# Banded attention into an ELU feed-forward on one core: a planned order of the first transfers, and two leading 256-token tiles with x transposed on TensorE

## The chip, the core and the metric

One core of one Trainium2 chip runs the whole program. The metric is the device time in microseconds of one execution; a run's time holds the profiled span of the instructions and a little around it. Three runs of the kernel before took 389.42, 391.37 and 386.51 us.

## What is computed

Eight batches of eight heads, 576 tokens, head width 64, float32 inputs. Attention inside a band of 32 positions to either side, then the heads side by side as 4608 tokens of width 512, then a feed-forward with an ELU between two matrices (512 to 2048 to 512).

```python
scores = scale * np.matmul(q, k.transpose(0, 1, 3, 2))
mask = np.abs(pos[:, None] - pos[None, :]) <= 32
attn = softmax(np.where(mask, scores, -1e9))
x = np.matmul(attn, v).transpose(0, 2, 1, 3).reshape(4608, 512)
h = x @ w_in
g = np.where(h > 0.0, h, np.exp(np.minimum(h, 0.0)) - 1.0)
out = g @ w_out
```

## The kernel before

**Tiling.** A *pair* is 128 tokens (two query blocks of 64); there are 36. For a pair, QK (line 216, 16 small matmuls into psS), SM (line 227, exp on ACT), MK (line 239, the band mask on DVE, two instructions), AV (line 251, two groups of eight matmuls, with a column of ones that gives the row sum), RN (lines 264 and 266, reciprocal and multiply on DVE, once for each group, giving xs) and X (line 275, a DMA transpose on SP's queue from xs into xt). Four pairs make an FFN *tile* of 512 tokens, nine tiles in all (`sizes = [4] * 9`). For a tile, sixteen steps H (line 286, four matmuls 128x512 into psH), EX (line 294, exp on ACT), FF and GG (lines 300 and 305, on DVE), then Y (line 319, four parts of four matmuls for each 128 tokens), YC (line 325, ACT copy) and OUT (line 330, SP).

**Loads.** q and k of a batch come in four float32 transfers (line 151: k and q of four heads, then of the other four); batch 0's are issued on SP, later ones on ACT's queue. POOL casts them to bf16 (line 166; batch 0's are shared with ACT and DVE), PE transposes them (T, line 176), ACT and DVE copy them out (E, lines 189 and 191). v of a batch is five casting transfers on POOL's queue (lines 197 to 202), and two transfers on SP's queue (SV, lines 206 and 207) make a copy of v shifted by 64 partitions, which the odd query blocks read. w_in and w_out come in four chunks each (lines 351 and 356), also on POOL's queue. Chunk c of w_in serves steps 4c to 4c+3 of H; chunk c of w_out serves part c of Y.

**What sets the order.** `Plan` holds each operation with engine, duration, rank and dependences, simulates the engines and writes the instructions in the order of the simulated starts. It sets only the order on each engine; on the chip every engine works through its instructions in that order and waits on semaphores. In the planner a transfer takes `dma` on a clock of the queue that issued it, plus 1.8. Batch 1's q and k wait there for nothing but batch 0's casts, and batch 1's v for batch 1's last cast (`deps.append(("C", 1, "q", 1))`); the loads of batch b from 2 on wait for QK of six pairs earlier.

Of the kernel before, what the change touches and what calls it, by code (L numbers as in the profile page):

```python
# [20 lines left out]
class Plan:  # L21
# [8 lines left out]

    def op(self, name, eng, dur, rank, deps, fn, dma=0.0):
        self.ops[name] = (eng, dur, rank, tuple(deps), fn, dma)

    def run(self):
# [7 lines left out]
        free = {}  # L42
        ring = {}
        ready = {}
# [5 lines left out]
        while len(order) < len(ops):  # L50
# [9 lines left out]
            del ready[e][n]  # L60
            _, dur, _, _, fn, dma = ops[n]
            free[e] = t + dur
            if dma:
                ring[e] = max(ring.get(e, 0.0), t + dur) + dma
                end = ring[e] + 1.8
            else:
                end = t + dur
            done[n] = end
            order.append((t, n))
            for u in users.get(n, ()):  # L70
                left[u] -= 1
                if left[u] == 0:
                    ue = ops[u][0]
                    r = max(done[d] + (0.0 if ops[d][0] == ue
                                       and not ops[d][5] else self.LAT)
                            for d in ops[u][3])
                    ready.setdefault(ue, {})[u] = r
# [7 lines left out]
def kernel(  # L85
# [9 lines left out]
    nc = tc.nc  # L95
# [173 lines left out]
    def X(i):  # L269
        xs = live.pop(("X", i)).rearrange("p h d -> p (h d)")  # L270
        t, c = where[i]
        if c == 0:
            xts[t] = xtp.tile([128, NDO, tiles[t][1] * 128], BF16,
                              name="xt", tag="xt")
        nc.sync.dma_start_transpose(xts[t][:, :, c * 128:(c + 1) * 128], xs)

# [55 lines left out]

    sizes = [4] * 9
    tiles, where = [], {}
# [6 lines left out]
    NT = len(tiles)  # L341
    NC0 = sizes[0]

# [24 lines left out]
    engs = {"DVE": nc.vector, "ACT": nc.scalar, "POOL": nc.gpsimd}  # L368
    cdur = {"DVE": 1.2, "ACT": 1.5, "POOL": 1.5}
    for b in range(B):  # L370
        need = prank(b * NQB // 2)
        r0 = need - 60
        early = [("QK", b * NQB // 2 - 6)] if b > 1 else []
        for half in range(2):
            for nm in ("q", "k"):
                deps = list(early)
                if b:
                    deps.append(("C", b - 1, nm, half))
# [3 lines left out]
                         b, nm, half, nc.scalar if b else nc.sync),  # L382
                     dma=3.0)
                eng = casts0[nm, half] if b == 0 else "POOL"
# [102 lines left out]
    for n, (t, c) in enumerate(yseq):  # L487
# [80 lines left out]
```

## Time and profile before

| | us |
|---|---|
| three runs, median (lowest to highest) | 389.42 (386.51 to 391.37) |
| the profiled execution | 387.12 |
| its span | 385.3 |
| PE busy | 313.8 (81%) |
| DVE busy | 246.7 (64%) |
| ACT busy | 173.7 (45%) |
| POOL busy | 86.0 (22%) |

All numbers of the rows below are from that one execution, in us from the start of its span. A busy PE is not PE at its peak, since its clock has two levels; the views give the granted clock as a share of full speed. A name such as `xs<-psO` is the written tile, then the one read; an instruction on `SPq` or `ACTq` is the issue of a transfer, not the transfer. A wait for several semaphores is put down to the one that came last by the profile.

### The profile page before, as it was taken

The numbers are of one execution on the slowest core, as the hardware profiler recorded it, in microseconds if no ns is written. First come the engines' busy times: TensorE is split into PE (matmuls) and PEld (weight loads), VectorE is DVE, ScalarE is ACT, GpSimd is POOL, SyncE is SP. The second block draws the span as 40 slices with busy tenths as digits, with TensorE's granted clock in tenths as the row PEclk, the third lists the DMA queues.
The fourth block names the chain that finished last, engine by engine and source line by source line (L and its number), as shares of the span: only waits on it lengthen the run. The fifth ranks groups of instructions, "written<-read, shape, count | busy, mean of one in ns | idle before, by whom it ended". The sixth has DMA issues, their size and how long they took to land.

```text
span 385.3 us, 6794 instructions
## 1 busy us (share of the span) xinstructions
PE 313.8 (81%) x2643; PEld 162.7 (42%) x2688; DVE 246.7 (64%) x529; ACT 173.7 (45%) x274; POOL 86.0 (22%) x93
## 2 busy tenths in 40 slices
PE   1325306786799949999999999989999999999995
PEld 1214202343445515554555445445554444444442
DVE  5133303669878909769977897598778778766620
ACT  4142303562555415555555556365654554444321
POOL 7366331059300162004500370060000000000000
PEclk9999755968999989999999999999999999999999
DMA  8999999789971989279933994591211212111012
GB/s 190 227 208 217 187 183 183 154 170 101 150 143 57 201 202 76 43 173 229 108 77 80 210 180 100 128 201 43 68 43 44 53 43 70 42 43 54 27 56 82
DMA packets 83679, 46.64 MB, mean 121 GB/s; under 512 B 58560, under 2 KB 79040, under 8 KB 83648
## 3 DMA queue, kind: packets, MB, share of 16 engines
q0 software_dynamic: 41728, 8.92, 30.1%
q1 hardware_dynamic: 30720, 20.78, 24.0%
q10 hardware_dynamic: 11200, 16.52, 19.6%
q8 instruction: 21, 0.34, 0.4%
q14 instruction: 10, 0.08, 0.1%
HBM read 36.70 MB, written 9.44 MB: 120 GB/s over the span
## 4 chain that ended last, share of the span: by engine, by line
PE 61%; DMA 16%; DVE 10%; issue 4%; ACTq 2%; ACT 2%; POOL 2%; another core or an unknown queue 1%; SPq 0%; POOLq 0%
PE psH L286 28%; PE psY L319 23%; DMA vw<-in_v_dram 7%; DMA stg<-in_k_dram 5%; DMA xt<-xs 4%; PE psO L251 3%; PE psT L176 3%; DVE pm L239 3%; ACTq L151 2%; DVE f L300 2%; DVE g L305 2%; PE psS L216 2%; DVE xs L266 2%; POOL bf L166 1%; ACT pu L227 1%
## 5 line engine op out<-in xcount | busy, mean ns | idle before, releaser
L286 PE MATMUL psH<-xt,w_in_sb 128*128 128x512 bf16 x558 | 149.9, 391 | 27.7 <-DMA vw<-in_v_dram 16.9
L294 ACT ACTIVATE e<-psH 128x512 f32<-128x512 f32 x144 | 86.0, 599 | 138.6 <-PE psH L286 121.0
L319 PE MATMUL psY<-w_out_sb,g 128*128 128x512 bf16 x502 | 131.0, 379 | 1.9 <-issue 0.6
L300 DVE TENSOR_SCALAR f<-e 128x512 bf16<-128x512 f32 x144 | 69.0, 479 | 70.5 <-ACT e L294 70.3
L305 DVE TENSOR_TENSOR g<-psH,f 128x512 bf16<-128x512 f32 x144 | 99.4, 690 | 4.5
L286 PEld LDWEIGHTS <-w_in_sb 128*128 128x128 bf16 x576 | 55.1, 100 | 90.0 <-issue 13.6
L166 POOL CAST bf<-stg 96x1536 bf16<-96x1536 f32 x29 | 43.8, 1513 | 159.2 <-DMA stg<-in_k_dram 142.0
L319 PEld LDWEIGHTS <-g 128*128 128x128 bf16 x576 | 52.0, 98 | 52.3 <-issue 0.3
L227 ACT ACTIVATE pu<-psS 128x1024 bf16<-128x1024 f32 x36 | 36.8, 1022 | 17.4 <-PE psS L216 11.8
L239 DVE TENSOR_TENSOR pm<-pu,masks 128x512 bf16<-128x512 bf16 x72 | 35.5, 534 | 13.7 <-ACT pu L227 13.7
L251 PE MATMUL psO<-vw,pm 128*128 128x65 bf16 x544 | 30.0, 196 | 13.4 <-DMA vw<-vw 9.3
L251 PEld LDWEIGHTS <-pm 128*128 128x128 bf16 x576 | 27.4, 101 | 29.9 <-issue 9.7
L176 PE MATMUL psT<-ident,bf 96*128 96x96 bf16 x348 | 27.0, 219 | 9.9 <-ACT kT L189 5.7
L176 PEld LDWEIGHTS <-bf 96*128 96x128 bf16 x384 | 23.4, 108 | 27.4 <-issue 8.8
L266 DVE TENSOR_TENSOR xs<-psO,rc 128x256 bf16<-128x256 f32 x68 | 28.8, 424 | 7.2 <-DMA xt<-xs 4.7
L325 ACT COPY y<-psY 128x512 f32<-128x512 f32 x33 | 19.4, 588 | 14.7 <-PE psY L319 14.1
L189 ACT COPY qT<-psT 128x576 bf16<-128x576 bf16 x30 | 19.2, 640 | 13.3 <-PE psT L176 7.9
L264 DVE RECIPROCAL rc<-psO 128x4 f32<-128x4 f32 x68 | 12.0, 177 | 15.9 <-PE psO L251 15.3
L200 POOL DMA_DIRECT2D vw<-in_v_dram x24 | 21.2, 896 | 2.5 <-PE psT L176 2.5
L216 PE MATMUL psS<-qT,kT 64*128 64x64 bf16 x576 | 16.2, 199 | 5.2 <-ACT qT L189 3.6
L216 PEld LDWEIGHTS <-kT 64*128 64x128 bf16 x576 | 11.6, 99 | 18.8 <-issue 18.3
L189 ACT COPY kT<-psT 128x576 bf16<-128x576 bf16 x21 | 13.5, 641 | 10.3 <-issue 6.6
(39 smaller groups left out, 61.2 us busy)
## 6 DMA issues: line engine op xcount, KB each, us to landing
out_dram<-y SPq DMA_DIRECT2D x36, 256.0 KB, 2.0
stg<-in_k_dram ACTq DMA_DIRECT2D x14, 576.0 KB, 9.5
stg<-in_q_dram ACTq DMA_DIRECT2D x14, 576.0 KB, 10.0
vw<-vw SPq DMA_DIRECT2D x16, 260.0 KB, 4.3
vw<-in_v_dram POOLq DMA_DIRECT2D x24, 128.0 KB, 5.5
w_in_sb<-in_moe_w_in_dram POOLq DMA_DIRECT2D x4, 512.0 KB, 14.7
w_out_sb<-in_moe_w_out_dram POOLq DMA_DIRECT2D x4, 512.0 KB, 30.9
vw<-in_v_dram POOLq DMA_DIRECT2D x16, 96.0 KB, 5.4
```

What stands on the lines that cost most here:

```text
L166: eng.tensor_copy(dst, src)
L176: nc.tensor.transpose(pt[:, j, :], src[:, j, 2 * hp:2 * hp + 2, :], ident[0:PR, 0:PR])
L216: nc.tensor.matmul(psS[:, h % 2, s, hp, :], lhsT=kT[b % NKB][base:base + 64, hp, qb * QB:qb * QB + 128], rhs=qT[b % NKB][base:base + 64, h ...
L227: nc.scalar.activation(pu, live.pop(("S", i)), AX.Exp, scale=SCALE)
L239: nc.vector.tensor_mul(dst, pu[:, :, s], mb)
L251: nc.tensor.matmul(o[:, j, :], lhsT=p[:, h, s * QB:s * QB + 128], rhs=vw[b % NVB][:, qb, h, :], start=(s == 0), stop=(s == 1))
L266: nc.vector.tensor_mul(live["X", i][:, g * HP:(g + 1) * HP, :], o[:, :, 0:D], rb)
L286: nc.tensor.matmul(ps, lhsT=w_in_sb[:, do, fo * 128:(fo + 1) * 128], rhs=xts[t][:, do, :], start=(do == 0), stop=(do == NDO - 1))
L294: nc.scalar.activation(e, ps, AX.Exp)
L300: nc.vector.tensor_scalar(f, e, -1.0, 0.0, ALU.add, ALU.min)
L305: nc.vector.tensor_tensor(gs[t][:, fo, :], ps, f, ALU.max)
L319: nc.tensor.matmul(ps, lhsT=gs[t][:, fo, c * 128:(c + 1) * 128], rhs=w_out_sb[:, fo, :], start=(fo == 0), stop=(fo == NFO - 1))
```

## The change

The planner gets one clock for all transfers that carry `dma`, a fixed delay (`lag`) for others, and an earliest end (`at`) for the first loads, so its times for the first 60 us come from a table. Batch 1's q and k depend on SM of pair 0; batch 1's v depends on batch 0's last cast on POOL and no longer on batch 1's; w_in no longer depends on batch 0's v, and its rank stands before that of batch 1's v. The loads of a batch from 2 on depend on step 8 of H two tiles before the tile in which the batch begins. The tiles become two of 256 tokens and eight of 512. For the first four pairs X is four PE transposes into psT and one DVE copy (XE) into xt; the other 32 stay DMA transposes.

```diff
+            end = max(end, at)
...
+        dst = xts[t][:, :, c * 128:(c + 1) * 128]
+        if i >= NC0:
+            nc.sync.dma_start_transpose(dst, xs)
+            return
+        pt = psT_p.tile([128, NDO, 128], BF16, name="psT", tag="psT")
+        for do in range(NDO):
+            nc.tensor.transpose(pt[:, do, :], xs[:, do * 128:(do + 1) * 128],
+                                ident)
+        live["XT", i] = (dst, pt)
+
+    def XE(i):
+        dst, pt = live.pop(("XT", i))
+        nc.vector.tensor_copy(dst, pt)
...
-    sizes = [4] * 9
+    sizes = [2, 2] + [4] * 8
...
-    NC0 = sizes[0]
+    NC0 = 4
...
+    LAND = {(0, "k", 0): 6.2, (0, "q", 0): 8.2, (0, "k", 1): 10.5,
+            (0, "q", 1): 13.0, (1, "k", 0): 27.0, (1, "q", 0): 31.0,
+            (1, "k", 1): 35.0, (1, "q", 1): 39.0}
...
-        early = [("QK", b * NQB // 2 - 6)] if b > 1 else []
+        t0 = where[b * NQB // 2][0]
+        early = [("H", max(t0 - 2, 0), 15 if t0 == 2 else 8)] if b > 1 else []
...
+                if b == 1:
+                    deps.append(("SM", 0))
...
-            deps.append(("C", 1, "q", 1))
...
+            deps.append(("C", 0, "k", 1))
...
-        P.op(("WI", c), "POOL", 1.0, -900 + c,
-             [("C", 0, "k", 1), ("LV", 0)], lambda c=c: WI(c), dma=5.0)
+        P.op(("WI", c), "POOL", 1.0, -990 + c,
+             [("C", 0, "k", 1)], lambda c=c: WI(c),
+             at=(19.5, 24.0, 28.5, 33.0)[c])
...
-        P.op(("X", i), "SP", 0.1, r + 3, deps, lambda i=i: X(i), dma=0.6)
+        if i < NC0:
+            if i:
+                deps.append(("X", i - 1))
+            P.op(("XT", i), "PE", 0.3, r + 3, deps, lambda i=i: X(i))
+            P.op(("X", i), "DVE", 0.42, r + 3, [("XT", i)],
+                 lambda i=i: XE(i))
+        else:
+            P.op(("X", i), "SP", 1.2, r + 3, deps, lambda i=i: X(i), lag=4.0)
```

On POOL, from behind the issue of batch 0's v (`vw_105`) to the end of the issue of batch 1's v (`vw_106`), the kernel before has:

```order
L166 CAST bf<-stg 96x4x6x64 [waits DMAHW2_49]
L166 CAST bf<-stg 96x4x6x64 [waits DMAHW4_49]
L351 DMA w_in_sb<-in_moe_w_in_dram 128x4x512 x3
L351 DMA w_in_sb<-in_moe_w_in_dram 128x4x512 [waits DMASW0_49]
L166 CAST bf<-stg 96x4x6x64 [waits DMAHW5_49]
L166 CAST bf<-stg 96x4x6x64 [waits DMAHW7_49]
L166 CAST bf<-stg 96x4x6x64 [waits DMAHW1_49]
L197 DMA vw_106<-in_v_dram 96x8x64 [waits DMASW1_49,DVE_49]
L200 DMA vw_106<-in_v_dram 128x8x64 [waits DMASW2_49]
L200 DMA vw_106<-in_v_dram 128x8x64 [waits DMASW3_49]
L200 DMA vw_106<-in_v_dram 128x8x64 [waits DMASW4_49]
L202 DMA vw_106<-in_v_dram 96x8x64 [waits DMASW5_49]
```

The first cast is batch 0's, the other four are batch 1's. Now, from the same place (line 170 is the cast, 367 w_in, 201 to 206 v):

```order
L170 CAST bf<-stg 96x4x6x64 [waits DMAHW2_49]
L367 DMA w_in_sb<-in_moe_w_in_dram 128x4x512 x3
L367 DMA w_in_sb<-in_moe_w_in_dram 128x4x512 [waits DMASW0_49]
L201 DMA vw_106<-in_v_dram 96x8x64 [waits DMASW1_49,DVE_49]
L204 DMA vw_106<-in_v_dram 128x8x64 [waits DMASW2_49]
L204 DMA vw_106<-in_v_dram 128x8x64 [waits DMASW3_49]
L204 DMA vw_106<-in_v_dram 128x8x64 [waits DMASW4_49]
L206 DMA vw_106<-in_v_dram 96x8x64 [waits DMASW5_49]
L170 CAST bf<-stg 96x4x6x64 [waits DMAHW6_49]
L170 CAST bf<-stg 96x4x6x64 [waits DMAHW7_49]
L170 CAST bf<-stg 96x4x6x64 [waits DMAHW0_49]
L170 CAST bf<-stg 96x4x6x64 [waits DMAHW2_49]
```

Batch 1's four casts moved behind w_in and behind batch 1's v; the four chunks of w_out follow these rows in both.

On PE, at the first FFN matmul of the program, the kernel before has batch 1's last transposes and then:

```order
L176 LDWEIGHTS bf
L176 MATMUL psT<-ident,bf 128x96
L286 LDWEIGHTS w_in_sb [waits DMAHW4_49,DMAHW6_49,DMAHW2_49,DMASW5_49]
L286 MATMUL psH<-xt,w_in_sb 128x512 [waits DMAHW1_49]
L286 LDWEIGHTS w_in_sb
```

Now AV of pair 2 stands ahead of it (line 255), and it needs pairs 0 and 1 only:

```order
L255 LDWEIGHTS pm_108
L255 MATMUL psY<-vw_105,pm_108 128x65
L302 LDWEIGHTS w_in_sb [waits DMASW5_49]
L302 MATMUL psH<-xt,w_in_sb 128x256 [waits DVE_49]
L302 LDWEIGHTS w_in_sb
```

The waits for the four DMA transposes (the DMAHW ones) are gone; a wait for DVE, which copies xt, and the one for w_in's first chunk are left. Batch 1's transposes T now stand between steps of H of the first two tiles.

On PE shortly before the first step of H of the tile of pairs 4 to 7 (the second tile before, the third now), there is now, behind a part of Y, a transpose of batch 2 that waits for POOL's cast:

```order
L335 LDWEIGHTS g
L335 MATMUL psY<-w_out_sb,g 128x512
L180 LDWEIGHTS bf [waits Pool_49]
L180 MATMUL psT<-ident,bf 128x96 [waits Activation_49]
L180 LDWEIGHTS bf
```

It is T of heads 4 and 5, which needs the last of batch 2's four loads; in the kernel before, all of batch 2's transposes stood among the steps of the first tile, and parts of Y stand in this place.

## Rows read from the trace of the kernel before

**Rows 1.** Busy time by engine in three stretches (PE, PEld, DVE, ACT, POOL, PEclk, DMA, GB/s).

```profile
0.00:61.35 61.35, 15.18 (x225) 12.52 (x226) 16.83 (x43) 15.19 (x20) 30.54 (x43) 0.85 1.35 197
61.35:106.10 44.75, 34.77 (x363) 18.46 (x369) 32.15 (x67) 23.35 (x36) 18.79 (x19) 0.83 1.45 153
200.00:320.00 120.00, 116.17 (x1008) 59.02 (x1024) 94.38 (x201) 63.35 (x102) 16.58 (x13) 1.00 0.49 102
```

**Rows 2.** Timeline, start to 107 us: start, us, engine, line, instruction [idle before <-releaser].

```profile
14.31 0.95 DVE L166 CAST bf<-stg 96x1536 bf16<-96x1536 f32 x1
...
33.39 0.54 PE L251 MATMUL psO<-vw,pm 128*128 128x65 bf16 x7 [9.35 <-DMA vw<-vw]
...
33.97 0.18 DVE L264 RECIPROCAL rc<-psO 128x4 f32<-128x4 f32 x1 [8.81 <-PE psO L251]
...
37.49 0.42 DVE L266 TENSOR_TENSOR xs<-psY,rc 128x256 bf16<-128x256 f32 x1
...
61.35 0.58 PE L286 MATMUL psH<-xt,w_in_sb 128*128 128x512 bf16 x1 [16.86 <-DMA vw<-in_v_dram]
...
106.10 1.24 PE L286 MATMUL psH<-xt,w_in_sb 128*128 128x512 bf16 x4 [1.23 <-DMA xt<-xs]
```

**Rows 3.** Tile view of xt, 35 to 49, then 86 to 105: issues, times to landing.

```profile
L275 SPq DMA_TRANSPOSE xt<-xs x4: 1205/1264/1659, 35.2 to 46.8; - x4
...
DMA to landing us min/median/max: 10.5/13.7/17.5
...
L275 SPq DMA_TRANSPOSE xt<-xs x5: 1189/1191/1203, 86.9 to 104.8; - x5
...
DMA to landing us min/median/max: 4.2/6.1/6.4
```

**Rows 4.** Tile views of vw (one v load alone; first shift) and of w_in_sb.

```profile
L200 POOL DMA_DIRECT2D vw<-in_v_dram x3: 880/892/896, 85.2 to 87.0; - x3
...
DMA to landing us min/median/max: 3.5/4.8/6.0
...
L206 SPq DMA_DIRECT2D vw<-vw x1: 710/710/710, 24.4 to 24.4; - x1
...
DMA to landing us min/median/max: 6.8/7.5/8.2
...
L351 POOL DMA_DIRECT2D w_in_sb<-in_moe_w_in_dram x4: 760/766/780, 18.8 to 21.0; - x4
...
DMA to landing us min/median/max: 10.2/14.7/17.5
```

**Rows 5.** Timeline rows of single DVE, PE and POOL instructions.

```profile
46.71 0.74 DVE L191 COPY kT<-psT 128x576 bf16<-128x576 bf16 x1
...
63.88 0.43 DVE L300 TENSOR_SCALAR f<-e 128x512 bf16<-128x512 f32 x1 [16.42 <-ACT e L294]
64.34 0.69 DVE L305 TENSOR_TENSOR g<-psH,f 128x512 bf16<-128x512 f32 x1
64.95 0.75 DVE L239 TENSOR_TENSOR pm<-pu,masks 128x512 bf16<-128x512 bf16 x2
...
68.31 0.42 PE L176 MATMUL psT<-ident,bf 96*128 96x96 bf16 x6
...
80.83 1.12 DVE L300 TENSOR_SCALAR f<-e 128x512 bf16<-128x512 f32 x1 [0.80 <-ACT e L294]
...
86.82 3.58 DVE L239 TENSOR_TENSOR pm<-pu,masks 128x512 bf16<-128x512 bf16 x2
```

**Rows 6.** POOL's timeline beside these: a cast, and the issue of v.

```profile
80.20 1.47 POOL L166 CAST bf<-stg 96x1536 bf16<-96x1536 f32 x1 [20.61 <-DMA stg<-in_k_dram]
...
85.22 2.64 POOL L200 DMA_DIRECT2D vw<-in_v_dram  x3
```

**Rows 7.** Batch 4's loads: first issue on ACT's queue, and POOL's last cast of them.

```profile
127.73 0.32 ACTq L151 DMA_DIRECT2D stg<-in_k_dram  x1
...
141.59 1.47 POOL L166 CAST bf<-stg 96x1536 bf16<-96x1536 f32 x1 [1.74 <-DMA stg<-in_q_dram]
```

More of the change, by code (lines that the diff above doesn't have):

```diff
@@ L29, in __init__, with op @@
         self.ops = {}
-    def op(self, name, eng, dur, rank, deps, fn, dma=0.0):
-        self.ops[name] = (eng, dur, rank, tuple(deps), fn, dma)
+    def op(self, name, eng, dur, rank, deps, fn, dma=0.0, lag=0.0,
+           at=0.0):
+        self.ops[name] = (eng, dur, rank, tuple(deps), fn, dma, lag, at)
     def run(self):
@@ L42, in run @@
         free = {}
-        ring = {}
+        server = 2.0
         ready = {}
@@ L60, in run @@
             del ready[e][n]
-            _, dur, _, _, fn, dma = ops[n]
+            _, dur, _, _, fn, dma, lag, at = ops[n]
             free[e] = t + dur
             if dma:
-                ring[e] = max(ring.get(e, 0.0), t + dur) + dma
-                end = ring[e] + 1.8
-            else:
-                end = t + dur
+                server = max(server, t + dur) + dma
+                end = server + 2.0
+            else:
+                end = t + dur + lag
+            end = max(end, at)
             done[n] = end
@@ L74, in run @@
                     r = max(done[d] + (0.0 if ops[d][0] == ue
-                                       and not ops[d][5] else self.LAT)
+                                       and not (ops[d][5] or ops[d][6] or ops[d][7]) else self.LAT)
                             for d in ops[u][3])
@@ L274, in X @@
                               name="xt", tag="xt")
-        nc.sync.dma_start_transpose(xts[t][:, :, c * 128:(c + 1) * 128], xs)
+        dst = xts[t][:, :, c * 128:(c + 1) * 128]
[10 more added lines that the diff above has]
+        nc.vector.tensor_copy(dst, pt)
     gs, es, ys = {}, {}, {}
@@ L382 @@
                          b, nm, half, nc.scalar if b else nc.sync),
-                     dma=3.0)
+                     dma=0.0 if b < 2 else 2.2, lag=2.0,
+                     at=LAND.get((b, nm, half), 0.0))
                 eng = casts0[nm, half] if b == 0 else "POOL"
@@ L397 @@
         if b == 1:
-            deps.append(("C", 1, "q", 1))
-        P.op(("LV", b), "POOL", 4.5, (-2000, -899)[b] if b < 2 else r0, deps, lambda b=b: load_v(b), dma=8.0)
+            deps.append(("C", 0, "k", 1))
+        P.op(("LV", b), "POOL", 4.5, (-2000, -899)[b] if b < 2 else r0, deps, lambda b=b: load_v(b),
+             dma=5.0 if b > 1 else 0.0, at=(17.0, 45.0)[b] if b < 2 else 0.0)
         P.op(("SV", b), "SP", 0.2, need - 20, [("LV", b)],
-             lambda b=b: shift_v(b), dma=2.0)
+             lambda b=b: shift_v(b), lag=4.5)
         for hp in range(HP):
@@ L420 @@
     for c in range(NWC):
-        P.op(("WI", c), "POOL", 1.0, -900 + c,
-             [("C", 0, "k", 1), ("LV", 0)], lambda c=c: WI(c), dma=5.0)
+        P.op(("WI", c), "POOL", 1.0, -990 + c,
+             [("C", 0, "k", 1)], lambda c=c: WI(c),
+             at=(19.5, 24.0, 28.5, 33.0)[c])
         P.op(("WO", c), "POOL", 1.0, -890 + c, [("C", 1, "q", 1)],
-             lambda c=c: WO(c), dma=5.0)
+             lambda c=c: WO(c),
+             at=(50.0, 54.0, 58.0, 62.0)[c])
     for i in range(NPAIR):
@@ L504 @@
         P.op(("OUT", t, c), "SP", 0.06, r, [("YC", t, c)],
-             lambda t=t, c=c: OUT(t, c), dma=1.0)
+             lambda t=t, c=c: OUT(t, c), lag=2.5)
     with tc.manual_schedule():
```

## The prediction, made before the changed kernel ran

> **What bounds the kernel now.** I read the busy time by stretch first. From 200 to 320 us PE is busy 116.17 of 120 at full clock [rows 1]: there PE sets the pace, and this change takes no work from it. So the question is when that dense state begins. Up to 61.35 PE is busy 15.18 us; from 61.35 to 106.10 it is busy 34.77 of 44.75 at a granted clock of 0.83, so partly at 1.2 GHz, with DVE busy 32.15 [rows 1]. Next the timeline: AV of pair 0 starts at 33.39, after 9.35 us of waiting for the shifted v; the first FFN matmul starts at 61.35 after 16.86 us of waiting; the second tile's at 106.10 [rows 2]. The profile puts the wait at 61.35 down to v, but the row of that matmul in the order shows its semaphores: DMA transposes of x and w_in. The tile view of xt says which: the four transposes were issued from 35.2 to 46.8 and took 10.5 to 17.5 us to land, against 4.2 to 6.4 for those after 86 [rows 3]. They ran beside batch 1's v, w_out and batch 2's q and k.
>
> I therefore follow two moments: H0, the first FFN matmul (61.35), and T2, the first step of H of pairs 4 to 7 (106.10). At T2 about the same work is left on PE in both kernels: counted in the order, the changed one has 3 more parts of Y behind it and 3 QK and 6 T fewer, some 3 us each way. From 106.10 to the end of the span are 385.3 - 106.10 = 279.2 us, and the run's time is 387.12 - 385.3 = 1.8 more. So time = T2 + 281.0, plus what later loads add.
>
> **The change part by part.**
>
> *First loads, to AV of pair 0.* Batch 1's q and k no longer run beside batch 0's v. Batch 0's q and k have landed by 14.31, where their last cast starts [rows 2]; v alone lands 3.5 to 6.0 us after its issue [rows 4], and its issue stands first on POOL, long before that cast. So v is there between 14.3 and 20.3; I take 17, nearer the low end since its packets are queued by then. The shift took 6.8 to 8.2 us to land [rows 4] and is two issues of 0.7; AV of pair 0 starts at 25 (22 to 29), not 33.39.
>
> *From there to H0.* Pair 1's xs was ready at 37.91 in the kernel before, 4.5 us behind its first AV [rows 2]. Now one PE transpose group and one DVE copy follow. Neither is in the trace. Six 96-column transposes take 0.42 [rows 5], so four of 128 columns cost between 0.28 and 0.6; the copy is nearest to the DVE copy of 576 columns, 0.74 [rows 5], so between 0.37 and 0.74. With 0.5 and 0.67, H0 = 25 + 4.5 + 1.2 = 30.7, say 31. w_in's first chunk is needed then. Its issue now stands ahead of batch 1's casts, so no later than the 18.8 to 21.0 of before, and the chunks took 10.2 to 17.5 us [rows 4]: the first by 29, the fourth by 38.5, and that one serves step 12, past 40. Not on the path.
>
> *From H0 to T2, by DVE.* An FFN step costs DVE 0.43 + 0.69 at 512 tokens [rows 5]. At 256 the nearest row for the second is the multiply of the same kind over 256 columns, 0.42 [rows 2]; the same fixed part gives 0.29 for the first. So 0.71 a step (bounds 0.56, half, and 1.12, no gain), 32 steps: 22.7. RN of pairs 2 to 7 is 12 groups of 0.18 + 0.42 [rows 2]: 7.2. MK of five pairs at 0.75: 3.75; two copies into xt 1.3; one copy of kT 0.74 [rows 5]. Sum 35.7. Before, DVE was busy 32.15 of 44.75, or 72%, in the stage that answers to this [rows 1]; at that pace 35.7 becomes 49.6. I take 40, nearer the low end, because the stage of before ended in a wait for x of some 4 us behind the last issue, and the order now leaves five parts of Y between. T2 = 31 + 40 = 71. PE, busy 34.77 before and about 38 with the three more parts of Y, fits in.
>
> *From H0 to T2, by loads.* The order puts T of batch 2's heads 4 and 5 ahead of T2; it waits for the last of batch 2's casts. These loads are issued on ACT behind step 7 of tile 1, some 24 of the 32 steps in, at about 31 + 23/35.7 x 40 = 57. Batch 4's four loads took 143.06 - 127.73 = 15.3 us from first issue to the end of the last cast [rows 7]. So this T runs at about 72, with POOL's issue of batch 2's v ahead of that cast, and T2 is 72 to 75. What waits behind it on PE is the last of tile 0's and tile 1's Y and T2 itself. I take T2 = 73.
>
> *Work added off the path.* Sixteen more EX on ACT cost at most 16 x 0.6, and ACT is half idle. SP loses four transposes, which blocked nothing else.
>
> *Later batches.* Loads now start nearer to their use. Counted on ACT from the last load to the first E of heads 4 and 5: 14 EX before, 8 to 10 now. From T2 on 128 steps are left, so 279.2/128 = 2.2 us a step, and 8 steps are 17 us against the 15.3 of [rows 7]. I add 1 in all (0 to 6).
>
> Sum: 73 + 281.0 + 1 = **355**. Against the profiled execution's 387.12 that is 32 less; the median of the three runs lies 2.3 above that execution, so the same figure is 34 below it.
>
> **The rivals.**
>
> 1. *DVE and loads faster (343 to 349).* If the small steps cost half (0.56), DVE's 35.7 becomes 31 and T2 is 62 with no waits; 343. For it: nothing else that I see is on the path. Against: it also needs batch 2's loads to land in under 10 us.
>
> 2. *POOL holds DVE, or transposes starve again (359 to 367).* FF beside a cast took 1.12 against 0.43, MK beside the issue of v 3.58 against 0.75 [rows 5, 6]. Four casts fell into this stage before, eight do now, with three issues of transfers on POOL. At 0.7 for a cast and 2.8 for an issue that is 5.6 + 8.4 = 14 on the 35.7: T2 = 31 + 49.7 = 80.7, time 362. The Trainium skill, "SBUF — State Buffer", section "Who interferes with whom", says that a DVE instruction in a two-port mode, and one with two SBUF inputs against a reading GpSimd one, is blocked for the whole GpSimd instruction, and that DVE operations of other kinds are not; the two rows agree, and by it the steps that read PSUM would not suffer. The other way here: the transposes of pairs 4 to 7 are still DMAs and now run beside batch 2's q and k. Pair 7's would be issued near 66; with the 10.5 to 17.5 of [rows 3] T2 is 77 to 84, time 359 to 366. The Trainium skill, "DMA: Bandwidth & Descriptors", section "Queues, rings and completion order", says that each DMA engine goes round between the queues with work, packet by packet; by that rule the planner's single clock orders nothing between ACT's queue and SP's, and the slow landings of [rows 3] agree.
>
> 3. *Batch 1 stays late (368 to 381).* If w_in and batch 1's q and k, sharing the engines, push batch 1's v to 61, where the wait for it ended before [rows 2], the shift lands at 69 and AV of pair 5 starts there. Behind it stand some 14 of the 40 us, 17 at the pace of before: T2 86, time 368, and more if w_out, behind v on its queue, is late as well. Against: 197 GB/s up to 61.35 [rows 1] went partly into batch 2's loads and w_out, which now stand behind.
>
> 4. *No change (382 to 397).* The DMA wait was not what held the first tile. The four transposes' landings end where H0 starts, which speaks against it.
>
> 5. *Slower.* The later loads, now gated half a tile before their use, come late in each of batches 2 to 7: PE stands in order behind T. From 34 us of gain, 5.7 us for each of six batches bring it back to even, 7 us make it slower by 2%. For it: the margin above is about 2 us. Against: a load would have to take 21 us from issue to cast.
>
> **How the numbers follow.** About 2% is what a measurement here can tell from no change. Forecast (350 to 358): 0.45. Rival 1: 0.15. Rival 2: 0.28. Rival 3: 0.05, no change 0.03, slower 0.04. The range 343 to 367 takes the first three and leaves about 0.12 out; narrowed to 8 in 10 it would cut through the middle of a rival. Faster by over 2% (below 381.6) are the forecast and rivals 1 to 3: 0.93.
>
> **What would show it.** In the changed profile: AV of pair 0 at 22 to 29; the first 128x256 FFN matmul near 31, waiting for DVE and not for a DMA; DVE above 85% busy from there to the first 128x512 step; that step at 70 to 76, behind a T that waited for POOL; PE dense afterwards. The forecast is wrong if the shift of batch 0's v or w_in lands much later than said, if the first 512-token step waits for x, or if PE waits for T in every later batch.

## The result and the profile after

Four runs of the changed kernel took 367.38 us in the median (366.73 to 368.16), four of the kernel before beside them 387.97: ratio 0.950, 95% interval 0.942 to 0.958, so 5.0% faster. The forecast was 355, with a range of 343 to 367: the direction was right, six tenths of the gain came (20.6 of 33), and the median lies 0.4 above the range. The profiled execution took 366.73, its span 364.8. Medians and ranges here are of all executions; the ratios leave out slow ones, those more than 1.5% above the fastest of their kernel.

Busy time in three stretches of the kernel after (columns as in [rows 1]), cut at the first FFN matmul and at the first step of H of pairs 4 to 7:

```profile
0.00:36.12 36.12, 11.29 (x169) 9.35 (x169) 13.49 (x37) 11.03 (x13) 19.06 (x33) 1.00 1.37 218
36.12:83.76 47.64, 37.59 (x429) 25.72 (x433) 36.11 (x105) 24.22 (x51) 24.29 (x25) 0.96 1.58 169
...
200.00:320.00 120.00, 116.35 (x975) 59.03 (x993) 93.76 (x202) 63.84 (x101) 13.01 (x9) 1.00 0.41 93
```

H0 is 36.12 instead of 61.35, T2 83.76 instead of 106.10; the stretch from 200 on is as in [rows 1]. The granted clock of 1.00 up to 36.12 does not fit the rows: eight matmuls of 128x256 at H0 took 1.86, eight at 52.30 took 1.04, so PE still went at about half pace at H0. The timeline of the kernel after, with the rows that answer to [rows 2], and what stands around T2:

```profile
18.16 0.38 ACTq L155 DMA_DIRECT2D stg<-in_k_dram  x1
...
18.34 0.71 SPq L210 DMA_DIRECT2D vw<-vw  x1
...
30.12 0.55 PE L255 MATMUL psO<-vw,pm 128*128 128x65 bf16 x7 [7.45 <-DMA vw<-vw]
...
36.12 1.86 PE L302 MATMUL psH<-xt,w_in_sb 128*128 128x256 bf16 x8
...
52.30 1.04 PE L302 MATMUL psH<-xt,w_in_sb 128*128 128x256 bf16 x8
...
57.18 0.32 ACTq L155 DMA_DIRECT2D stg<-in_k_dram  x1
...
60.58 7.12 SPq L281 DMA_TRANSPOSE xt<-xs  x3
...
69.51 0.66 PE L180 MATMUL psT<-ident,bf 96*128 96x96 bf16 x6 [3.15 <-POOL bf L170]
...
74.02 0.42 DVE L270 TENSOR_TENSOR xs<-psO,rc 128x256 bf16<-128x256 f32 x1 [3.19 <-DMA xt<-xs]
74.37 1.85 DVE L243 TENSOR_TENSOR pm<-pu,masks 128x512 bf16<-128x512 bf16 x2
...
77.25 1.20 SPq L281 DMA_TRANSPOSE xt<-xs  x1
...
77.47 1.49 DVE L316 TENSOR_SCALAR f<-e 128x256 bf16<-128x256 f32 x1
...
80.69 0.42 PE L255 MATMUL psO<-vw,pm 128*128 128x65 bf16 x8 [1.87 <-DVE xs L270]
...
83.76 1.89 PE L302 MATMUL psH<-xt,w_in_sb 128*128 128x512 bf16 x8
```

The shift of batch 0's v is issued at 18.34, 0.2 behind batch 1's first q/k load, and AV of pair 0 starts 11.8 later. Near 70 three things stand together: T of batch 2 waits for POOL's cast; RN of pair 7 waits until the transpose of pair 4 has read its xs (`xsp` has three buffers); and the transpose of pair 7 can be issued only behind that, at 77.25, and lands just ahead of T2. The tile view of xt, 55 to 86, has the landings:

```profile
L281 SPq DMA_TRANSPOSE xt<-xs x5: 1191/1206/1304, 60.6 to 81.8; - x5
...
DMA to landing us min/median/max: 6.1/10.0/13.4
```

60.58 + 13.4 = 74.0, where RN of pair 7 goes on; 77.25 + 6.1 = 83.4, 0.4 ahead of T2. The row of T2 shows no wait for it. PE's last long wait ahead of T2 is that of AV at 80.69, for DVE, which from 74.02 on works through what the wait of RN held up, MK (1.85) and FF (1.49) beside a busy POOL among it. So two paths behind the same wait end within 0.4 us of each other. (A row with x3 spans from the first issue to the end of the last: the 7.12 is no landing time. Where an expectation below gives 7.1 or 16.9 us for such transposes, it took a span for one.)

### The profile page after: what moved, and what is told of

Read it like the earlier page. It is cut to its first block, busy times and chain, and to the rows that moved or that the text cites. A ratio compares the mean times of both kernels' runs of the same rounds, so it can differ in the third digit from the quotient of the medians.

```text
span 364.8 us, 7010 instructions
## 1 busy us (share of the span) xinstructions
PE 314.2 (86%) x2725; PEld 168.9 (46%) x2768; DVE 252.9 (69%) x565; ACT 177.2 (49%) x290; POOL 86.1 (24%) x93
## 4 chain that ended last, share of the span: by engine, by line
PE 58%; DVE 18%; DMA 14%; issue 3%; ACTq 2%; POOL 2%; ACT 1%; SPq 1%; POOLq 0%; DVEq 0%
PE psY L335 24%; PE psH L302 24%; DMA vw<-vw 6%; DVE g L321 6%; DVE f L316 6%; DMA xt<-xs 5%; DVE pm L243 4%; PE psO L255 4%; DMA vw<-in_v_dram 3%; PE psT L180 2%; DVE xs L270 2%; ACTq L155 2%; PE psS L220 2%; PE psO L335 1%; PE psS L335 1%
## 5 line engine op out<-in xcount | busy, mean ns | idle before, releaser
L302 PE MATMUL psH<-xt,w_in_sb 128*128 128x512 bf16 (+1 forms) x624 | 147.3, 360 | 4.5 <-DVE g L321 2.4
L310 ACT ACTIVATE e<-psH 128x512 f32<-128x512 f32 (+1 forms) x160 | 88.1, 555 | 115.9 <-PE psH L302 90.1
L316 DVE TENSOR_SCALAR f<-e 128x512 bf16<-128x512 f32 (+1 forms) x160 | 75.7, 473 | 45.8 <-ACT e L310 45.7
L321 DVE TENSOR_TENSOR g<-psH,f 128x512 bf16<-128x512 f32 (+1 forms) x160 | 102.0, 637 | 5.1
L302 PEld LDWEIGHTS <-w_in_sb 128*128 128x128 bf16 x640 | 60.4, 99 | 61.2 <-issue 6.1
L231 ACT ACTIVATE pu<-psS 128x1024 bf16<-128x1024 f32 x36 | 36.8, 1021 | 12.7 <-PE psS L220 10.3
L243 DVE TENSOR_TENSOR pm<-pu,masks 128x512 bf16<-128x512 bf16 x72 | 34.0, 514 | 4.8 <-ACT pu L231 4.8
L180 PE MATMUL psT<-ident,bf 96*128 96x96 bf16 x348 | 25.4, 211 | 7.0 <-POOL bf L170 3.6
L268 DVE RECIPROCAL rc<-psO 128x4 f32<-128x4 f32 x68 | 12.1, 178 | 22.0 <-PE psO L255 21.5
L204 POOL DMA_DIRECT2D vw<-in_v_dram x24 | 21.3, 900 | 15.5 <-PE psO L255 15.3
L206 POOL DMA_DIRECT2D vw<-in_v_dram x8 | 6.5, 812 | 41.4 <-PE psO L255 40.6
```

The costliest lines, as they stand in the source:

```text
L180: nc.tensor.transpose(pt[:, j, :], src[:, j, 2 * hp:2 * hp + 2, :], ident[0:PR, 0:PR])
L231: nc.scalar.activation(pu, live.pop(("S", i)), AX.Exp, scale=SCALE)
L243: nc.vector.tensor_mul(dst, pu[:, :, s], mb)
L302: nc.tensor.matmul(ps, lhsT=w_in_sb[:, do, fo * 128:(fo + 1) * 128], rhs=xts[t][:, do, :], start=(do == 0), stop=(do == NDO - 1))
L310: nc.scalar.activation(e, ps, AX.Exp)
L316: nc.vector.tensor_scalar(f, e, -1.0, 0.0, ALU.add, ALU.min)
```

## Experiments

All are single edits or sums of edits of the kernel after. The planner simulates anew for each, so an edit of one dependence can also change the order on other engines; where a run below hangs on that, it is said. H0 and T2 are the two moments in the profiled execution; with 512-token tiles T2 is the first step of the second tile.

| run | edit | median (range) | ratio to before, 95% | H0 | T2 | span |
|---|---|---|---|---|---|---|
| after | | 367.38 (366.73–368.16) | 0.942–0.958 | 36.1 | 83.8 | 364.8 |
| e1_dma_x | x by DMA | 372.98 (372.15–374.01) | 0.958–0.970 | 44.0 | 87.3 | 370.4 |
| e2_tiles512 | 9 x 512 | 364.93 (362.08–367.07) | 0.934–0.952 | 39.4 | 82.7 | 361.8 |
| e3_old_gate | old gate, batch 2 on | 374.08 (371.97–380.66) | 0.957–0.972 | 35.6 | 93.5 | 372.0 |
| e15_b1_early | batch 1 not gated | 369.16 (368.26–370.95) | 0.948–0.963 | 41.1 | 85.7 | 366.5 |
| e4_late_b1 | batch 1 later | 374.9 (373.93–376.32) | 0.960–0.973 | 32.2 | 86.4 | 372.2 |
| e5_v0_direct | direct v, ahead of cast | 367.91 (364.76–369.04) | 0.940–0.954 | 30.5 | 79.8 | 366.3 |
| e13_v0_late | direct v, behind cast | 368.09 (366.78–370.88) | 0.944–0.961 | 30.2 | 83.2 | 365.5 |
| e6_b2_step2 | batch 2 at step 2 | 373.73 (372.63–374.29) | 0.955–0.969 | 35.8 | 90.3 | 371.2 |
| e7_x8_pe | 8 pairs' x on PE | 364.79 (362.72–368.41) | 0.930–0.946 | 35.9 | 82.3 | 361.6 |
| e10_x8_step2 | e6 + e7 | 367.73 (366.96–369.61) | 0.945–0.957 | 35.9 | 82.4 | 365.3 |
| e16_xs5 | 5 xs buffers | 369.48 (362.75–371.20) | not given | 36.9 | 81.3 | 360.9 |
| e19_warm | PE kept busy | 366.39 (366.05–367.84) | 0.939–0.949 | 35.7 | 84.4 | 365.9 |
| e11_t512_x8 | e2 + e7 | 361.52 (358.50–365.92) | 0.926–0.943 | 40.2 | 85.1 | 364.1 |
| e12_t512_x8_v0 | e11 + e13 | 364.96 | 0.935–0.951 | 38.9 | 75.7 | 362.4 |
| e17_t512_x8_g10 | e11, batch 2 earlier | 363.32 (362.39–365.89) | 0.930–0.942 | 39.5 | 85.0 | 360.9 |
| e18_t512_x8_g10_v0 | e17 + e13 | 360.51 (360.29–360.87) | 0.923–0.933 | 38.5 | 83.0 | 358.9 |

One of the four executions of e12 lay at 1126.69, for a reason that nothing here shows; the other three at 364.3 to 365.1. Where two intervals overlap, they do not settle the order of the two kernels. Those of e1, e3 and e6 overlap that of the kernel after by 0.003 at most, and there every execution is slower (371.97 or more) than any of the kernel after (368.16 or less).

### Which part of the change carries the gain

**x by DMA transposes again.**

```diff
-        if i >= NC0:
+        if i >= NXT:     # NXT = 0, here and where the plan adds XT
```

> The kernel after, with x of the first four pairs by DMA transposes again; order of the loads and the 256-token tiles kept. Theory (the PE transposes are part of what moves H0, since a DMA transpose beside w_in and batch 1's q and k lands after 10.5 to 17.5 us in the kernel before and the last three of pairs 4 to 7 took 7.1 us to land in the kernel after): AV of pair 0 still at 30.1, H0 at 43 to 50 instead of 36.1, T2 at 88 to 95 and the time 371 to 378. Rival (by 30 us w_in has mostly landed, the transposes land in about 4 us and spare DVE four copies of 0.41): H0 at 40, T2 at 84 to 86, time 367 to 369.

5.6 us slower than after. Its timeline, then the tile view of xt from 30 to 60:

```profile
44.03 2.72 PE L302 MATMUL psH<-xt,w_in_sb 128*128 128x256 bf16 x12 [7.20 <-DMA xt<-xs]
```

```profile
L281 SPq DMA_TRANSPOSE xt<-xs x4: 1189/1198/1282, 31.9 to 41.5; - x4
...
DMA to landing us min/median/max: 8.4/9.2/9.7
```

AV of pair 0 still starts at 30.12, so the transposes alone hold H0 back, by 7.9; at T2 3.5 of it are left. H0 and the time are in the theory's ranges; T2 (87.29) is 0.7 below its range.

**512-token tiles.**

```diff
-    sizes = [2, 2] + [4] * 8
+    sizes = [4] * 9
```

> The kernel after with nine tiles of 512 tokens, so that the first step of H waits for four pairs instead of two; x of the first four pairs stays on PE and the loads stay in order. Theory (the half tile brings H forward by about 7 us, but its 32 steps cost DVE 32 x 0.70 = 22.4 instead of 16 x 1.12 = 17.9, so 4.5 of it is given back where DVE is busy): first H at 43, first step of the second tile 2 to 4 later than T2 of the kernel after (86 to 88), time 369 to 371. Rival 1 (the 7 us are kept in full, because DVE has slack): time 373 to 376. Rival 2 (T2 is set by batch 2's casts and the transposes of pairs 4 to 7, not by the FFN behind them): 366 to 368.

The numbers of the theory fell: H0 comes 3.2 later and not 7, T2 1.0 earlier, and the median is 2.4 lower, with intervals that overlap. PE's first step of the second tile waits 3.83 for a DMA transpose, which is rival 2's reason, though the time lies below its range too. The four pairs' x is ready soon after the second, so a half tile starts little sooner, and its 32 small steps cost DVE more. The 256-token tiles bring no gain that can be seen here.

**The old gate for batch 2 and later.**

```diff
-        early = [("H", max(t0 - 2, 0), 15 if t0 == 2 else 8)] if b > 1 else []
+        early = [("QK", b * NQB // 2 - 6)] if b > 1 else []
```

> The kernel after with the old dependence for the loads of batch 2 and later (QK of six pairs earlier, instead of step 8 of H two tiles earlier). Theory (gating keeps batch 2's loads off the queue while w_out, batch 1's shift and the first transposes of pairs 4 to 7 need it): the loads are issued near 40 to 50, batch 1's shift takes over 9 us instead of 8, transposes of pairs 4 to 7 take over 10 us, T2 at 86 to 92, time 370 to 376. Rival (the gate only makes batch 2 late: T of batch 2 waits 3.2 for POOL's cast in the kernel after): T2 at 79 to 81, time 362 to 365.

6.7 slower, in the theory's range, but what goes wrong first is something else. Its timeline:

```profile
36.71 0.32 ACTq L155 DMA_DIRECT2D stg<-in_k_dram  x1
...
46.37 2.88 POOL L170 CAST bf<-stg 96x1536 bf16<-96x1536 f32 x2 [13.90 <-DMA stg<-in_k_dram]
...
93.47 4.43 PE L302 MATMUL psH<-xt,w_in_sb 128*128 128x512 bf16 x12 [5.43 <-DMA xt<-xs]
```

Batch 2's first load is issued at 36.71 and lands 9.5 later, at 46.2. That is what POOL waits 13.90 for: with the gate gone the plan puts batch 2's first cast ahead of batch 1's third. Batch 1's loads had landed by 39.0, as in the kernel after, where their last two casts ran at 36.4 and 39.4; here these casts stand behind the wait, and w_out behind them is issued at 52.4 instead of 40.8. So the cost begins with an order on POOL. Whether the earlier loads crowd other transfers too, as the theory had it, is not separated here; T2 is 1.5 above its range.

**Batch 1 not gated by SM of pair 0.**

```diff
-                if b == 1:
-                    deps.append(("SM", 0))
```

> The kernel after without the dependence of batch 1's q and k on SM of pair 0, so they are issued on ACT's queue between the copies of batch 0 (planned 9 to 15 us, not 18 to 21), beside batch 0's v; everything else stays. Theory (this order carries a good part of the gain, because v of batch 0 shares the queue with them): v of batch 0 and its shift land at 32 to 35 instead of 30.1, H0 at 38 to 41, T2 at 85 to 89, time 369 to 373. Rival (whatever lands first, the same bytes have to land before H0, and batch 1's casts come earlier): AV of pair 0 at 29 to 31, time 366 to 368.

```profile
35.95 0.54 PE L255 MATMUL psO<-vw,pm 128*128 128x65 bf16 x7 [14.50 <-DMA vw<-vw]
...
41.08 1.86 PE L302 MATMUL psH<-xt,w_in_sb 128*128 128x256 bf16 x8
```

Five us later at H0, as the theory has it, but 1.9 at T2 and 1.8 in the median, with intervals that overlap: right in its place, and most of the loss is made good before the end. The undone parts together (5.6 + 6.7 + 1.8, less 2.4) would come to 11.7 of the 20.6 that the change brought, if they add and if the 1.8 and the 2.4, which are not settled, are taken as they stand; the rest was not taken apart (w_in ahead of batch 1's v and the new table of times were never undone alone).

### Does the time follow H0?

**Batch 1 later still**, until SM of pair 3.

```diff
-                    deps.append(("SM", 0))
+                    deps.append(("SM", 3))
```

> Batch 1's four loads on ACT's queue are moved behind SM of pair 3, which runs only after AV of pair 0; nothing else on ACT, POOL or SP moves. In the changed kernel the shift of batch 0's v was issued at 18.34 and AV of pair 0 started at 30.12, 11.8 us later, with batch 1's loads issued from 18.16. Theory (those loads take the shift's share of the DMA engines): the shift lands as in the kernel before, 6.8 to 8.2 us after its issue, AV of pair 0 starts at 26 to 27 and the first FFN matmul at 32 to 33 instead of 36.12. Rival (w_in, or the shift itself, is what is slow): AV of pair 0 stays at 29 to 31. For the total time both leave it open, 361 to 369, since batch 1 and w_out come 10 us later.

```profile
27.02 0.54 PE L255 MATMUL psO<-vw,pm 128*128 128x65 bf16 x7 [5.58 <-DMA vw<-vw]
```

The shift, issued at 17.96, is through 9.1 later instead of 11.8: batch 1's q and k beside it cost 2.7. In the kernel before it took 9.0, counted in the same way, from 24.4 to AV of pair 0 at 33.39. The price is paid behind: T of batch 1 waits 5.04 for its cast, and the time is 7.5 longer.

**Batch 0's odd v blocks loaded directly**, without a shift; four transfers on POOL, first ahead of batch 0's last cast, then behind it.

```diff
+            for qb in range(1, NQB, 2):
+                lo = qb * QB - WIN
+                nc.gpsimd.dma_start(out=vt[:, qb, :, 0:D], in_=vb[lo:lo + 128])
```

> Batch 0 gets no shift: the odd blocks of its v are loaded from DRAM by four more transfers on POOL's queue, right behind the five. Theory (the wait for the shift put off the first FFN matmul and everything behind it): v is complete at 21 to 24, AV of pair 0 there, first FFN matmul at 27 to 30 instead of 36.12, first 512-token step at 76 to 79 instead of 83.76, time 359 to 363 (from 367.4). Rival (the first 512-token step hangs on batch 2's loads and not on the start): the start moves as said, but that step stays after 81 and the time above 365.

> The kernel after with batch 0's odd v blocks loaded by four direct transfers on POOL behind its last cast of batch 0 and ahead of w_in, and no shift for batch 0. (Issued ahead of the cast these four delayed it from 12.0 to 16.1, and the time was 367.9.) Theory (the shift, 11.8 us from issue to landing, is what makes AV of pair 0 late): odd blocks there at 21 to 24, AV of pair 0 at 22 to 25, H0 at 30 to 33 unless w_in's first chunk, now issued 3 to 6 later, is the last to come; T2 at 79 to 82, time 361 to 365. Rival (H0 moves, but DVE and batch 2's casts hold T2, or what is won is given back behind T2 as in the run with direct v ahead of the cast): 366 to 368.

Ahead of the cast the fourth transfer waited 3.85 on POOL, and the cast behind it ran at 16.11 instead of 12.0; H0 was 30.45 all the same. Behind it, AV of pair 0 started at 23.92 and H0 was 30.20, 5.9 earlier than in the kernel after. Neither is faster. In the first, T2 comes 4.0 earlier (79.80), and this is lost behind T2, where PE waits 2.9 for a shift of v instead of 0.9. In the second T2 hardly moves, as its timeline and its stretches show:

```profile
30.20 1.86 PE L310 MATMUL psH<-xt,w_in_sb 128*128 128x256 bf16 x8 [1.32 <-DVE xt L299]
...
70.25 0.59 SPq L219 DMA_DIRECT2D vw<-vw  x1
...
72.76 1.25 SPq L289 DMA_TRANSPOSE xt<-xs  x1
...
72.78 0.42 DVE L278 TENSOR_TENSOR xs<-psO,rc 128x256 bf16<-128x256 f32 x1 [3.29 <-DMA xt<-xs]
...
83.19 1.89 PE L310 MATMUL psH<-xt,w_in_sb 128*128 128x512 bf16 x4 [5.90 <-DMA xt<-xs]
```

```profile
74.00:78.00 4.00, 3.28 (x14) 1.31 (x12) 1.96 (x4) 0.64 (x1) 4.00 (x5) 0.67 1.23 283
78.00:82.00 4.00, 0.00 (x0) 0.00 (x0) 0.00 (x0) 0.00 (x0) 3.94 (x4) 0.76 1.46 173
82.00:87.00 5.00, 3.81 (x15) 1.70 (x16) 1.12 (x2) 1.13 (x2) 0.00 (x0) 0.51 1.74 199
```

The transpose of pair 7 ends at the same place as in the kernel after, but on another path. Its xs was ready at 67.1; on SP the plan now has a shift of batch 3's v ahead of it, whose second half (70.25) had waited 4.1, so the transpose is issued at 72.76, lands 10.4 later, and PE waits 5.90 for it. (The wait of RN at 72.78 is pair 8's.) PE and DVE have run out of work by then and stand from 78 to 82; PE is granted 0.67 of its clock before that and 0.51 behind it. H0 by -5.9, T2 by -0.6, the median by +0.7: the time is near the rival's, its reason (DVE and the casts) is not what held T2. Together with e5 (H0 -5.7, T2 -4.0, median +0.5) and e15 (+5.0, +1.9, +1.8): T2 follows H0 with anything from a tenth to seven tenths of its move, depending on what else the new order does, and no move of the time is clear of the noise.

### What holds T2

**Batch 2's loads at step 2 instead of 8**, **x of eight pairs on PE**, and both.

```diff
-        early = [("H", max(t0 - 2, 0), 15 if t0 == 2 else 8)] if b > 1 else []
+        early = [("H", max(t0 - 2, 0), 2 if b == 2 else 8)] if b > 1 else []
...
-        if i >= NC0:
+        if i >= NXT:     # NXT = 8
```

> Only the planner's gate of batch 2's loads is moved, from step 8 to step 2 of the second tile; in ACT's order the loads come 6 EX earlier, so at about 52 instead of 57.18. Theory (PE waits in order behind T of batch 2, whose loads start too late): the 3.15 us wait of T for POOL's cast at 69.51 goes, the first 512-token step comes at 77 to 80 instead of 83.76, time 361 to 364. Rival (the DMA transposes of pairs 4 to 7 beside these loads hold DVE's RN, whatever the loads' start): that step stays at 82 to 85, time 366 to 369.

> x of pairs 4 to 7 also goes through PE and DVE (four more groups of four transposes and a copy of 0.42 us each) instead of four DMA transposes. Theory (batch 2's loads set the first 512-token step): no gain, that step at 82 to 85, time 366 to 369. Rival (the DMA transposes, 3.19 us of waiting of RN at 74.02): the wait goes, the step comes at 79 to 81, time 363 to 365.

> The kernel after with two edits together: batch 2's loads gated by step 2 of H instead of step 8 (alone: 373.7, T of batch 2 at 64.4 but transposes of pairs 4 to 7 landing after 16.9 us and T2 at 90.2), and x of the first eight pairs on PE (alone: 364.8, T2 at 82.3). Theory (the earlier loads cost only through the transposes that they slow down, and those are gone): T of batch 2 at 64 to 65, T2 at 76 to 79, time 358 to 362. Rival (the earlier loads hurt w_out, batch 1's shift or batch 1's casts as much, or DVE is then the limit up to T2): T2 at 82 to 88, time 365 to 371.

Earlier loads alone cost 6.4. T of batch 2 comes 5 earlier, but the plan then puts it and its wait ahead of the last pairs; the transpose of pair 7 is issued at 79.77, behind a shift of v on SP that stands behind it in the kernel after, and T2 is 90.25, after 5.04 of waiting for it:

```profile
78.34 0.61 SPq L210 DMA_DIRECT2D vw<-vw  x1
...
79.05 0.60 SPq L211 DMA_DIRECT2D vw<-vw  x1
...
79.77 4.78 SPq L281 DMA_TRANSPOSE xt<-xs  x2
...
90.25 2.29 PE L302 MATMUL psH<-xt,w_in_sb 128*128 128x512 bf16 x5 [5.04 <-DMA xt<-xs]
```

The tile view of xt from 55 to 92 has the landings:

```profile
DMA to landing us min/median/max: 5.1/7.2/10.3
```

The longest is that of pair 7: 79.77 + 10.3 = 90.1. It was issued 2.5 later than in the kernel after and took 4.2 longer to land. So my theory for this run (loads too late) fell, and so did the reading in e10's expectation that the transposes of pairs 4 to 7 took up to 16.9: those of pairs 4 to 6 landed after 5.1 to 7.3. With x on PE the waits for transposes are gone and the median is 2.6 lower, overlapping. With both, T of batch 2 runs at 64.23 and no DMA transpose is waited for, and T2 is 82.35 as with e7: the rival's range. T at 64.23 has still waited 3.79 for POOL's cast, and behind it DVE and PE are both nearly full:

```profile
66.00:72.00 6.00, 5.45 (x71) 4.09 (x69) 5.30 (x13) 3.26 (x6) 6.00 (x7) 0.76 1.69 105
72.00:78.00 6.00, 4.99 (x57) 3.43 (x57) 5.41 (x18) 3.08 (x6) 5.84 (x7) 1.00 1.53 114
```

DVE is busy 10.7 of 12 and PE 10.4, at a granted clock of 0.76 in the first half, beside a POOL that is busy throughout; which of them sets T2 here is not shown. My reading is that three limits end near the same moment: the chain through xs and the transposes, batch 2's casts with T, and DVE's sum. Taking the first away moves T2 by 1.5, easing the second makes it later, and both together move it by 1.4.

**Five buffers for xs.**

```diff
-    xsp = ctx.enter_context(tc.tile_pool(name="xsp", bufs=3))
+    xsp = ctx.enter_context(tc.tile_pool(name="xsp", bufs=5))
```

> The kernel after with five buffers for xs instead of three, nothing else. In the kernel after RN of pair 7 waited 3.2 (74.02) until the transpose of pair 4 had read its xs, so the transpose of pair 7 was issued at 77.25 and the first 128x512 step ran at 83.76. Theory (the chain xs buffer, transpose of about 6 to 10, first step sets T2): RN of pair 7 has no DMA wait, its transpose is issued at 73 to 75, T2 at 79 to 82, time 362 to 365. Rival (batch 2's casts and T hold the same place on PE): the wait is gone but T2 at 83 to 84, time 366.5 to 368.

Not settled. In the profiled execution (362.75) RN of pair 7 has no DMA wait, its transpose is issued at 75.30 and T2 is 81.27, nearly as the theory has it; the other three executions took 368.92 to 371.20, at granted clocks of 0.982 to 0.991 against 0.995, and their traces are not at hand.

**PE kept busy in the wait for batch 2's and 3's casts.**

```diff
+        if b in (2, 3) and (nm, hp) == ("q", 0):
+            for r in range(40):
+                nc.tensor.transpose(pt[0:PR, r % TPP, :], ident[0:PR, 0:PR],
+                                    ident[0:PR, 0:PR])
```

> The kernel after with 40 extra transposes of the identity on PE (96 columns, written into psT and overwritten) ahead of the first transpose of batch 2 and again of batch 3, where PE waits for POOL's cast with its clock falling to 0.50 afterwards (70 to 73 and 117 to 120). They need nothing but psT. Theory (each of these waits costs a second time, because PE goes on at half clock): the granted clock stays at 1.00 there and the time falls by 2 to 4, to 363 to 366. Rival (PE is not the limit in these stretches, or the extra work delays what stands behind): clock at 1.00 or not, time 367 to 369.

The stretches of the kernel after, then of this one:

```profile
66.00:70.00 4.00, 0.85 (x11) 0.58 (x9) 1.77 (x5) 0.38 (x1) 2.70 (x2) 0.92 1.52 200
70.00:73.00 3.00, 3.00 (x23) 1.75 (x21) 0.18 (x1) 1.02 (x2) 1.26 (x1) 0.54 1.15 162
```

```profile
68.00:72.00 4.00, 3.95 (x67) 3.46 (x67) 2.61 (x7) 1.40 (x3) 1.46 (x1) 1.00 1.36 167
72.00:75.00 3.00, 0.34 (x7) 0.19 (x5) 0.40 (x2) 1.13 (x2) 2.65 (x3) 1.00 1.47 171
75.00:79.00 4.00, 3.92 (x25) 2.11 (x26) 3.97 (x8) 1.02 (x2) 4.00 (x5) 0.62 1.68 157
```

In the kernel after, PE does 0.85 us of work in 4 and then goes at about 1.2 GHz for 3. The filler holds the clock there; the next gap, 72 to 75, brings the same fall behind it, and T2 is 84.4. The median is 1.0 lower with overlapping intervals, so neither the theory's 2 to 4 nor its price was shown.

### Sums of edits

> Nine tiles of 512 tokens and x of the first eight pairs on PE. With 512-token tiles alone (364.9) the first step of the second tile, at 82.74, waited 3.8 for a DMA transpose while DVE was busy 2.3 of 6 us (72 to 78) and 0 of 6 (78 to 84). Theory (up to T2 the kernel with 512-token tiles is limited by the DMA transposes of pairs 4 to 7 alone): T2 at 78 to 80, time 358 to 362. Rival (the four extra PE transposes stand behind T in psT and those wait for POOL's casts, or what is won before T2 is lost behind it): T2 may fall, the time stays at 363 to 366.

> All three: 512-token tiles, x of the first eight pairs on PE, and batch 0's odd v blocks by direct transfers behind the cast. Theory (three separate delays ahead of T2, which add): AV of pair 0 at 22 to 25, first H at 33 to 35, T2 at 74 to 77, time 354 to 359. Rival (one limit under them, batch 2's casts at 61 to 76, holds T2): T2 at 78 to 82, time 360 to 364.

> 512-token tiles, x of the first eight pairs on PE, and batch 2's loads gated by step 10 of H of the first tile instead of step 15, with its four casts on POOL ahead of the issues of v. (Without the earlier gate: 361.5, loads issued at 58, casts at 63 to 78.) Theory (batch 2's casts are the last of three limits ahead of the second tile): loads at 51 to 53, casts done by 70, first step of the second tile at 76 to 79, time 356 to 360. Rival (DVE, with w_out and batch 1's shift delayed by the loads, takes over): first step at 80 or later, time 361 to 366.

> The same, and batch 0's odd v blocks by direct transfers behind the cast (alone on the kernel after: H0 at 30.2 instead of 36.1, but 368.1, since what was won went into a wait at 78 to 83 and a clock of 0.50 behind it). Theory (with transposes, tile size and casts out of the way the earlier start is kept): 352 to 357. Rival (the start is not kept, PE waits for batch 2 instead): 358 to 364.

The edits are the ones above; e17 and e18 gate batch 2 by step 10 of the first tile instead of 15 (`10 if t0 == 2 else 8`). e11 lies in its theory's range in the median; its profiled execution was its slowest and shows T2 at 85.1, so the theory's reason was not seen. e12 has T2 at 75.66, right on the theory, and yet a median 1.0 above even the rival's range: T of batch 3 waits 3.00 at 99.12, and PE goes at a clock of 0.50 from 98 to 104. e17 shows the rival: batch 2's loads are issued at 51.89, PE stands from 60 to 64 and goes at 0.57 up to 72. e18 is the fastest kernel of the study, ratio 0.928 (0.923 to 0.933), 1.9% below the kernel after, with its interval clear of that one's. Its time falls in the rival's range, not in the theory's: an early AV (23.84) does not make an early H0 (38.45) here, since T of batch 1 stands in between on PE and waits there for its cast (1.54 at 32.63), and the gain comes to 2.8 over e17. Its stretches:

```profile
0.00:38.45 38.45, 15.23 (x211) 12.52 (x213) 16.81 (x47) 12.50 (x16) 24.38 (x38) 0.92 1.75 209
38.45:83.00 44.55, 37.11 (x346) 20.04 (x352) 28.94 (x65) 21.81 (x35) 21.88 (x23) 0.92 1.51 186
```

DVE is busy 28.94 from H0 to T2 instead of 36.11, in 65 instructions instead of 105.

## Why the prediction was right and wrong

**Where the 12.4 us between 355 and 367.38 lie.** H0 came 5.1 later than forecast. From H0 to T2 it took 47.64 instead of 42, 5.6 more. From T2 to the end it took 1.0 more, and the median lies 0.65 above the profiled execution. Two steps failed: the shift of batch 0's v, and the waits between H0 and T2.

**What bounds the kernel, and that the dense state begins earlier: right.** The gain lies ahead of T2, and from T2 to the end of the span the kernel after takes 364.8 - 83.76 = 281.0, against 279.2 before and the 1 added for later loads.

**AV of pair 0 at 25 (22 to 29): wrong, 30.12.** v of batch 0 was taken as there at 17; the shift was issued at 18.34, 1.3 later. The larger error is the shift, for which 8 were taken and 11.8 came. The 6.8 to 8.2 of [rows 4] are those of its two transfers one by one; from the first issue to AV the kernel before took 9.0, so 1.0 is an error of reading. The other 2.8 come from the company: in the kernel before three of batch 1's four loads had been issued 12 us and more ahead of the shift. Batch 1's q and k now follow SM of pair 0, which falls at 18.16, the very moment of the shift, and with those loads moved away it took 9.1 (e4). The prediction counted what the change took from beside batch 0's v and not what it put beside its shift.

**From there to H0, 5.7: right** (6.0), and w_in was not waited for.

**DVE's sum from H0 to T2: right** to 0.4, in part by luck: 35.7 forecast, 36.11 busy. The steps cost 0.28 and 0.42 beside nothing, the copy of xt 0.41. But the sum put what POOL takes from DVE at nothing, and the 32 FF took 12.1 instead of 9.0, MK 4.8 instead of 3.75; RN of pair 8 came on top. Against it, DVE's instructions overlap at their ends: one by one they add up to 40.3, where 36.11 are covered. DVE was busy 76% of the stretch, not above 85%.

**The waits on top of it: wrong.** The sum allowed 4.3 and 2 more for T of batch 2; 11.5 came (47.64 - 36.11). DVE's waits in this stretch:

```profile
DVE rc L268 <- PE psO L255: 4.0, 4, 2.8
DVE xs L270 <- DMA xt<-xs: 3.2, 1, 3.2
DVE f L316 <- ACT e L310: 0.8, 2, 0.4
```

The longest of the first, 2.8, is T's wait for batch 2's cast, which holds AV in order on PE. The issue of its loads was forecast to 0.2 us (57.18). But the prediction had only T of heads 4 and 5 wait, just ahead of T2: that one ran at 81.80 and did not wait. The wait came at batch 2's first T, 69.51, which the sum has no term for, and it is time that DVE loses. The second was not forecast at all: three buffers of xs put the transposes of pairs 4 and 7 in series, 13.4 and 6.1 us. Rival 2 named slow transposes beside batch 2's loads, with T2 at 77 to 84; it is the rival nearest to what came, with H0 5 later as well, though the slow transpose was pair 4's and reached T2 through the buffers of xs. Its other half came too, in part: MK beside POOL's issue took 1.85 instead of 0.75, FF 1.49 instead of 0.28. GG, which reads PSUM, stayed at 0.41 to 0.42 throughout. The rule of the Trainium skill that the prediction cited ("SBUF — State Buffer", "Who interferes with whom") has it so for FF and GG, and these rows agree. For an instruction with two SBUF inputs, as MK is, it speaks of a GpSimd instruction that reads SBUF; that an issue of transfers slows MK too is shown by the 1.85 alone.

**time = T2 + 281, T2 = H0 + 42: the first held in the kernel after, the second not.** Over all runs with 256-token tiles, span minus T2 is 278.5 (e3) to 286.5 (e5), and e12 has 286.7: where T2 comes earlier, PE meets waits of later batches (2.9 for a shift of v in e5, 3.00 for batch 3's cast in e12). And T2 follows H0 only in part (e5, e13, e15). The sum treated H0 as a starting gun. In fact waits before T2, and behind it, fill up part of what H0 leaves. So the 5.1 by which H0 missed is not 5.1 of time that an earlier H0 would give back: none of the runs with an earlier H0 alone was faster. How the rest divides among transposes, casts and DVE is not settled: the run that takes the transposes away gains 2.6 with overlapping intervals, the run that brings the casts forward loses 6.4.

**The rivals.** Rival 1 did not come: a small step cost DVE 0.70, not 0.56. Rival 3 did not come: T of batch 1 was in time. Rival 5's fear, loads too late in every batch, did not come: from batch 1 on, PE's waits for POOL's casts are 3.6 in all, 3.1 of it at batch 2. Without the gate that it doubted the time was 6.7 longer (e3), though there the order on POOL changed as well. Rivals 4 and 5, no change and slower, are ruled out by the measured ratio.

## What to carry to other kernels

When the first matmul of a stage is brought forward, look for the next thing that does not move with it: the last transfer whose issue hangs on a buffer, or a load gated by a step further on. Put each moved transfer's own companions on the list, for the new time: a duration read where a transfer ran nearly alone does not hold where the change puts four more beside it. Before reading an experiment, read the new order on every queue: in e3, e6 and e13 the edit moved a cast or a shift of another batch ahead of what the run was about. Where several limits end within a few us, take them away in pairs before judging one.

## What was not expected of the hardware

A wait of PE was followed by a fall of its granted clock in several of these traces: 0.85 us of work in 4, then 0.54 for 3 us (kernel after); nothing in 4, then 0.51 for 5 (e13). So a wait can cost twice, though what the second part costs in the end was not shown (e19). Small matmuls cost PE no more for the same columns: four of 128x256 show 0.60 at full clock and four of 128x512 1.03, but eight of 128x256 in a row took 1.04 (52.30, kernel after), so a short group's figure holds an end that the next instruction overlaps. And executions of one kernel with the same instructions lay 8 us apart (e16, 362.75 to 371.20), more than most of the edits here are worth.
